# An fp32 product by Strassen's seven half-size products, in four column tiles of TensorE

## The chip, the cores and the metric

One core of a Trainium2 chip. The time is the device time of one execution in microseconds.

## The reference

```python
# x: (8, 4096, 192), weight: (8, 7); w_in: (192, 2048), w_out: (2048, 192); all fp32
w   = softmax(weight, axis=-1)
out = causal 7-tap convolution of x along the sequence, one filter per group of 24 channels
h   = out.reshape(32768, 192) @ w_in
g   = h * sigmoid(1.702 * h)
y   = g @ w_out                       # (32768, 192)
```

The two products are 25.8 billion multiply-adds, and both have to be fp32.

## The kernel before

VectorE makes the convolution for the next step while TensorE works on this one. A step has 1024 tokens: 512 of each half of the batch, one half on partitions 0 to 63 and the other on 64 to 127. The hidden product of this step and the output product of the step before are interleaved, both in row tiles of 64 rows. ("Tile" has two senses here: a buffer that the tile framework hands out from a pool, and a row or column tile, a part of TensorE's array.)

```python
TOK = 512; NF = 16; NC = 3; D = 192           # N_ST = 32 steps
psum_h = ctx.enter_context(tc.tile_pool(name="psum_h", bufs=2, space=PSUM))
psum_o = ctx.enter_context(tc.tile_pool(name="psum_o", bufs=2, space=PSUM))
...
def hidden(s, u):
    ph = psum_h.tile([P, 2, TOK], F32, name="ph")
    for c in range(NC):
        for h in range(2):
            nc.tensor.matmul(ph[:, h, :], w_in_s[halves[h], c, fc * P : (fc + 1) * P],
                             cts[s][halves[h], c, :], start=(c == 0), stop=(c == NC - 1))
    nc.scalar.activation(gs[s][:, fc, :, :], ph, AF.Gelu_apprx_sigmoid)

def output(s, u):                              # 16 such pieces a step
    ...
    if part == 0 and u % 2 == 0:
        acc[z2] = psum_o.tile([P, 2, TOK], F32, name="po")
    for fc in range(u % 2 * (NF // 2), (u % 2 + 1) * (NF // 2)):
        for a in range(2):
            nc.tensor.matmul(po[:, z, 0:D], gs[s][halves[a], fc, h, ...],   # stationary: tokens
                             w_out_s[halves[a], fc, :], ...)                # moving: 192 columns
    if part == 1 and u % 2 == 1:
        nc.vector.tensor_copy(osb[:, b : b + 2, :], po[:, :, 0:D])
        ...                                    # one store for 512 tokens
```

The output's accumulators are tiles of two PSUM banks, and the pool has two of them. While VectorE empties one, TensorE fills the other.

## Time and profile before

| | before |
|---|---|
| time | 2727.88 us (2727.16 to 2728.6) |
| TensorE busy | 98% of the span |
| a step of 1024 tokens | 83.46 us, of which hidden 41.3, output 41.6, the step's border 0.6 |
| first hidden product starts, second step starts | 32.6 us, about 94 us |

The lines behind this table stand in the prediction. A line of the costliest groups reads: line, engine, operation, tiles, shapes, count | busy us and mean ns of one | idle us before them and who ended it. A line of the chain reads: start us, duration us, what. PE is TensorE, PEld its weight loads, DVE VectorE, ACT ScalarE.

### The profile page before, as it was taken

What the parts mean: (1) busy time and instruction counts of PE and PEld (TensorE: products, weight loads), DVE (VectorE), ACT (ScalarE), POOL (GpSimd) and SP (SyncE); (2) the same over time, 40 slices, a digit from 0 to 9 for tenths busy, and PEclk for the clock granted to TensorE, in tenths of its full rate; (3) what the DMA queues carried; (4) which work ended last, traced back from release to release, by engine and by line L of the source; (5) the groups of instructions that cost most, each with busy time, mean ns of one, the idle gap of its engine ahead of it and who ended that gap; (6) DMA issues with size and microseconds to landing.
All of it is one profiled execution on the core that took longest, in us unless ns stands there. A gap on an engine that the chain in (4) does not pass through costs nothing.

```text
span 2725.4 us, 46647 instructions
## 1 busy us (share of the span) xinstructions
PE 2668.3 (98%) x22278; PEld 1927.5 (71%) x22278; DVE 638.7 (23%) x1001; ACT 533.6 (20%) x524; POOL 5.3 (0%) x15
## 2 busy tenths in 40 slices
PE   4999999999999999999999999999999999999999
PEld 2577777777777777777777777777777777777778
DVE  8412222122121222221221212222212222122200
ACT  2211211111111111111112111111111111111210
POOL 0000000000000000000000000000000000000000
PEclk9999999999999999999999999999999999999999
DMA  6111011110111110111101111101111011110000
GB/s 150 20 32 32 7 32 32 26 32 13 26 32 26 32 32 7 32 32 26 32 13 26 32 26 32 27 12 32 32 26 32 7 32 32 26 32 13 7 13 18
DMA packets 104045, 76.39 MB, mean 28 GB/s; under 512 B 3312, under 2 KB 101616, under 8 KB 103856
## 3 DMA queue, kind: packets, MB, share of 16 engines
q1 hardware_dynamic: 103072, 70.27, 12.0%
q8 instruction: 174, 2.85, 0.4%
q0 software_dynamic: 768, 3.15, 0.4%
q14 instruction: 15, 0.12, 0.0%
q10 hardware_dynamic: 16, 0.00, 0.0%
HBM read 48.23 MB, written 25.17 MB: 27 GB/s over the span
## 4 chain that ended last, share of the span: by engine, by line
PE 94%; DVE 5%; issue 0%; DMA 0%; SPq 0%; DVEq 0%
PE po L260 47%; PE ph L235 45%; DVE ct L224 2%; PE po L269 2%; DVE osb L277 1%; DVE g L161 0%; DVE g L154 0%; DMA xin<-in_x_dram 0%; DVE g L160 0%; DVE g L159 0%; DVE w_in_s L166 0%; DVE xt L207 0%; DVE g L158 0%; DVE g L152 0%; DVE g L153 0%
## 5 line engine op out<-in xcount | busy, mean ns | idle before, releaser
L260 PEld LDWEIGHTS po<-w_out_s,g 64*128 64x128 f32 x15872 | 1321.4, 187 | 234.3 <-issue 234.3
L235 PE MATMUL ph<-ct,w_in_s 64*128 64x512 f32 x6144 | 1417.1, 592 | 48.3 <-DVE w_in_s L166 26.3
L260 PE MATMUL po<-w_out_s,g 64*128 64x192 f32 x15872 | 1373.0, 323 | 0.0
L235 PEld LDWEIGHTS ph<-ct,w_in_s 64*128 64x128 f32 x6144 | 578.5, 188 | 554.4 <-issue 476.8
L242 ACT ACTIVATE g<-ph 128x1024 f32<-128x1024 f32 x512 | 524.3, 1024 | 2104.5 <-PE ph L235 2104.5
L277 DVE COPY osb<-po 128x384 f32<-128x384 f32 x128 | 71.3, 557 | 2057.1 <-PE po L260 2017.5
L224 DVE SCALAR_TENSOR_TENSOR ct<-xt,cw,ct 128x512 f32<-128x512 f32 x576 | 431.8, 750 | 16.0
L207 DVE STREAM_TRANSPOSE xt<-xin 128x512 f32<-128x512 f32 x96 | 60.5, 679 | 3.3 <-DMA xin<-in_x_dram 3.2
L222 DVE TENSOR_SCALAR ct<-xt,cw 128x512 f32<-128x512 f32 x96 | 45.0, 469 | 0.0
L269 PE MATMUL po<-w_out_s,g 128*128 128x192 f32 x256 | 41.9, 326 | 0.0
L269 PEld LDWEIGHTS po<-w_out_s,g 128*128 128x128 f32 x256 | 41.6, 190 | 0.2 <-issue 0.2
L179 ACT COPY w_in_s<-w_in_s 64x768 f32<-64x768 f32 x8 | 6.6, 830 | 37.9 <-DVE w_in_s L166 37.8
L154 DVE SCALAR_TENSOR_TENSOR g<-g 128x768 f32<-128x768 uint32 x8 | 7.7, 958 | 0.3
L161 DVE SCALAR_TENSOR_TENSOR g<-g 128x768 uint32<-128x768 uint32 x8 | 7.7, 958 | 0.3
L166 DVE SCALAR_TENSOR_TENSOR w_in_s<-g 64x768 f32<-64x768 f32 x8 | 7.6, 953 | 0.3
L195 PE MATMUL po<-e,sel 8*128 8x7 f32 x6 | 1.4, 354 | 4.9 <-DVE e L192 4.9
L195 PEld LDWEIGHTS po<-e,sel 8*128 8x128 f32 x6 | 1.3, 320 | 4.8 <-issue 4.8
L205 DVE COPY xt<-xt 128x18 f32<-128x18 f32 x28 | 4.7, 167 | 0.0
L160 DVE TENSOR_SCALAR g<-g 128x768 uint32<-128x768 uint32 x8 | 4.5, 560 | 0.3
L159 DVE TENSOR_SCALAR g<-g 128x768 uint32<-128x768 uint32 x8 | 4.5, 560 | 0.3
L158 DVE TENSOR_SCALAR g<-g 128x768 uint32<-128x768 uint32 x8 | 4.4, 554 | 0.0
L153 DVE TENSOR_SCALAR g<-g 128x768 uint32<-128x768 uint32 x8 | 4.4, 552 | 0.0
(19 smaller groups left out, 18.1 us busy)
## 6 DMA issues: line engine op xcount, KB each, us to landing
xin<-in_x_dram SPq DMA_DIRECT2D x128, 320.0 KB, 6.1
out_dram<-osb SPq DMA_DIRECT2D x62, 384.0 KB, 2.6
g<-in_moe_w_in_dram SPq DMA_DIRECT2D x8, 384.0 KB, 22.2
g<-in_moe_w_out_dram POOLq DMA_DIRECT2D x4, 768.0 KB, 16.7
out_dram<-osb SPq DMA_DIRECT2D x4, 192.0 KB, 2.0
w<-in_weight_dram ACTq DMA_DIRECT2D x1, 0.2 KB
```

The lines of the kernel that those rows point to most:

```text
L154: vec.scalar_tensor_tensor(out=m.bitcast(F32), in0=m_lo, scalar=2.0**-24, in1=m_hi, op0=ALU.mult, op1=ALU.add)
L161: vec.scalar_tensor_tensor(out=e, in0=hi, scalar=1 << 31, in1=e, op0=ALU.bitwise_and, op1=ALU.bitwise_or)
L166: vec.scalar_tensor_tensor(out=dst, in0=m[rows, :].bitcast(F32).rearrange("p (c n) -> p c n", c=c), scalar=2.0**-20, in1=e[rows, :].bitcas ...
L179: nc.scalar.copy(w_in_s[halves[1 - h], :, cols[h]], w_in_s[halves[h], :, cols[h]])
L207: nc.vector.transpose(xts[s][:, c, PAD:].rearrange("p (j t) -> p j t", t=Q), xins[s][:, :, c * R : c * R + Q],)
L222: nc.vector.tensor_scalar_mul(dst, src, tap)
L224: nc.vector.scalar_tensor_tensor(out=dst, in0=src, scalar=tap, in1=dst, op0=ALU.mult, op1=ALU.add)
L235: nc.tensor.matmul(ph[:, h, :], w_in_s[halves[h], c, fc * P : (fc + 1) * P], cts[s][halves[h], c, :], start=(c == 0), stop=(c == NC - 1),)
L242: nc.scalar.activation(gs[s][:, fc, :, :], ph, AF.Gelu_apprx_sigmoid)
L260: nc.tensor.matmul(po[:, z, 0:D], gs[s][halves[a], fc, h, (b + z) * P : (b + z + 1) * P], w_out_s[halves[a], fc, :], start=(part == 0 and ...
L269: nc.tensor.matmul(po[:, part, 0:D], gs[s][:, fc, h, (b + part) * P : (b + part + 1) * P], w_out_s[:, fc, :], start=(fc == 0), stop=(fc == ...
L277: nc.vector.tensor_copy(osb[:, b : b + 2, :], po[:, :, 0:D])
```

## The change

Its intent: the output product as 2 x 2 blocks (the tokens in two halves by batch, the 2048 hidden units and the 192 outputs in two halves each) by Strassen's scheme in Winograd's form, with 7 block products in place of 8. That is 1/8 fewer multiply-adds in the output product, still in fp32. For this the output weights become the stationary operand, in column tiles of 32: 96 outputs fill three tiles, and the fourth takes a quarter of the tokens for all three slices. The sums of g that the scheme needs, and the combinations of the products, are VectorE's. A step is now 512 tokens, first a hidden phase, then an output phase.

```diff
-    TOK = 512
+    T = 256;  TA = 3 * T // 4;  TB = T - TA;  TOK = 2 * T          # 64 steps of 512 tokens
-    psum_o = ctx.enter_context(tc.tile_pool(name="psum_o", bufs=2, space=bass.MemoryType.PSUM))
+    psum_o = ctx.enter_context(tc.tile_pool(name="psum_o", bufs=1, space=bass.MemoryType.PSUM))
...
+    def sums_g(s):
+        g = [gs[s][:, i, :, :] for i in range(NS)]
+        yield nc.vector.tensor_sub(g[T1], g[B12], g[B11])          # 128 x 2048 each
+        yield nc.vector.tensor_sub(g[T3], g[B22], g[B12])
+        yield nc.vector.tensor_sub(g[T2], g[B22], g[T1])
+        yield nc.vector.tensor_sub(g[T4], g[T2], g[B21])
...
+    def output(s, others):
+        po = psum_o.tile([P, NR, TOK], F32, name="po")             # NR = 4 banks, one tile
+        def product(a, b, bank, at, first=True):
+            dst = po[:, bank, at : at + TA]
+            for j in range(NK):                                    # 8 chunks
+                for c in range(3):
+                    nc.tensor.matmul(dst[c * Q : (c + 1) * Q, :],
+                        w_out_s[:, a, j, c * Q : (c + 1) * Q], g[:, b, j, 0:TA], ...)
+                for c in range(3):
+                    nc.tensor.matmul(dst[3 * Q :, c * TB : (c + 1) * TB],
+                        w_out_s[:, a, j, c * Q : (c + 1) * Q], g[:, b, j, TA:T], ...)
+            return dst
+        p1 = product(A11, B11, 0, 0)
+        next(others, None)                                         # one of the sums
+        vec.tensor_copy(u1, p1)
+        next(others, None)
+        p6 = product(S2, T2, 1, 0)
+        vec.tensor_add(u2, u1, p6)
+        next(others, None)
+        c11 = product(A12, B21, 0, 0, first=False)
+        turn(0, 0, c11)                                            # turn: 32x32 transposes
+        p7 = product(S3, T3, 2, 0)
+        vec.tensor_add(u3, u2, p7)
+        next(others, None)
+        p5 = product(S1, T1, 3, 0)
+        vec.tensor_add(v, u3, p5)
+        turn(1, 1, v)
+        vec.tensor_add(u2, u2, p5)
+        p3 = product(S4, B22, 1, TA)
+        vec.tensor_add(u2, u2, p3)
+        turn(0, 1, u2)
+        p4 = product(A22, T4, 2, TA)
+        vec.tensor_sub(u3, u3, p4)
+        turn(1, 0, u3)
...                                                                # 24 stores
+            if s == 1:                                             # after the second hidden phase
+                for i in range(NW):
+                    round_w_out(i)
+                sums_w_out()
```

(Left out: index changes of the hidden product, the scratch of the weight rounding, the stores.)

More of the change, by code (lines that the diff above doesn't have):

```diff
@@ L46 @@
     HF = F // 2
-    TOK = 512
-    NB = TOK // P
+    HD = D // 2
+    T = 256
+    TA = 3 * T // 4
+    TB = T - TA
+    TOK = 2 * T
     NJ = TOK // Q
     NF = F // P
+    NK = NF // 2
     PAD = K - 1
     CHUNKS = S // TOK
-    N_ST = (B // 2) * CHUNKS
+    N_BIG = (B // 2) * CHUNKS
+    N_ST = 2 * N_BIG
     XW = D - Q
-    assert B % 2 == 0 and D == NC * R and S % TOK == 0 and F % P == 0 and NF == 4 * NB
+    assert B % 2 == 0 and D == NC * R and HD == 3 * Q and S % TOK == 0 and F % (2 * P) == 0
     x_v = x.rearrange("(h p) s d -> h p s d", h=2)
@@ L64, with load_x @@
     g_pool = ctx.enter_context(tc.tile_pool(name="g", bufs=2))
+    u_pool = ctx.enter_context(tc.tile_pool(name="u", bufs=1))
     osb_pool = ctx.enter_context(tc.tile_pool(name="osb", bufs=2))
     psum_h = ctx.enter_context(tc.tile_pool(name="psum_h", bufs=2, space=bass.MemoryType.PSUM))
-    psum_o = ctx.enter_context(tc.tile_pool(name="psum_o", bufs=2, space=bass.MemoryType.PSUM))
+    psum_o = ctx.enter_context(tc.tile_pool(name="psum_o", bufs=1, space=bass.MemoryType.PSUM))
     ctx.enter_context(tc.manual_schedule())
-    xins, xts, cts, gs, acc = {}, {}, {}, {}, {}
+    xins, xts, cts, gs = {}, {}, {}, {}
     halves = [slice(0, R), slice(R, P)]
-    def load_x(s):
-        p, c = divmod(s, CHUNKS)
+    def load_x(big):
+        p, c = divmod(big, CHUNKS)
         xin = xin_pool.tile([P, NJ, XW], F32, name="xin")
@@ L86, in load_x, with new_g @@
                 )
-        xins[s] = xin
+        xins[big] = xin
+    NS = 7
+    B11, B12, B21, B22, T1, T2, T4 = range(NS)
+    T3 = B12
+    def new_g():
+        return g_pool.tile([P, NS, NK, T], F32, name="g")
     NW = 4
@@ L94 @@
     PIECE = NC * FW
-    assert PIECE == CW * D and 2 * NW * 2 * PIECE + 4 * PIECE <= NF * 2 * TOK
-    scratch = g_pool.tile([P, NF, 2, TOK], F32, name="g").rearrange("p f h t -> p (f h t)").bitcast(U32)
-    raw = scratch[:, 0 : 2 * NW * 2 * PIECE].rearrange("p (i n) -> p i n", i=2 * NW)
-    tmp = scratch[:, 2 * NW * 2 * PIECE : 2 * NW * 2 * PIECE + 4 * PIECE].rearrange(
-        "p (i n) -> p i n", i=4
-    )
+    assert PIECE == CW * D and FW == 2 * P and (NW * 2 + 4) * PIECE <= NS * NK * T
+    scratch = new_g().rearrange("p s f t -> p (s f t)").bitcast(U32)
+    raw = scratch[:, 0 : NW * 2 * PIECE].rearrange("p (i n) -> p i n", i=NW)
+    tmp = scratch[:, NW * 2 * PIECE : (NW * 2 + 4) * PIECE].rearrange("p (i n) -> p i n", i=4)
     w8 = consts.tile([H, K], F32)
@@ L109 @@
     w_in_s = consts.tile([P, NC, F], F32)
-    w_out_s = consts.tile([P, NF, D], F32)
     w_in_v = moe_w_in.bitcast(U32).rearrange("(c q) (h f) -> h q c f", q=R, h=2)
@@ L118 @@
             nc.sync.dma_start(out=piece[halves[h], :, :], in_=w_in_v[h, :, :, cols])
-    fc_order = [
-        (h * HF + i * FW) // P + j for i in range(NW) for h in range(2) for j in range(FW // P)
-    ]
+    A11, A12, A21, A22, S1, S2, S4 = range(NS)
+    S3 = A21
+    w_out_s = consts.tile([P, NS, NK, HD], F32)
     sel = consts.tile([H, NC, P], F32)
@@ L138 @@
             )
-    for i in range(NW):
-        nc.gpsimd.dma_start(
-            out=raw[:, NW + i, :].rearrange("p (c d) -> p c d", c=CW),
-            in_=w_out_v[:, i * CW : (i + 1) * CW, :],
-        )
     def round_piece(i, dsts):
@@ L163, in round_piece @@
         )
-        for rows, dst in dsts:
-            c = dst.shape[1]
+        for rows, c, cols, dst in dsts:
             vec.scalar_tensor_tensor(
                 out=dst,
-                in0=m[rows, :].bitcast(F32).rearrange("p (c n) -> p c n", c=c),
+                in0=m[rows, :].bitcast(F32).rearrange("p (c n) -> p c n", c=c)[:, :, cols],
                 scalar=2.0**-20,
-                in1=e[rows, :].bitcast(F32).rearrange("p (c n) -> p c n", c=c),
+                in1=e[rows, :].bitcast(F32).rearrange("p (c n) -> p c n", c=c)[:, :, cols],
                 op0=ALU.mult,
@@ L176, in round_w_in, with load_w_out, sums_w_out @@
         cols = [slice(h * HF + i * FW, h * HF + (i + 1) * FW) for h in range(2)]
-        round_piece(i, [(halves[h], w_in_s[halves[h], :, cols[h]]) for h in range(2)])
+        round_piece(
+            i, [(halves[h], NC, slice(0, FW), w_in_s[halves[h], :, cols[h]]) for h in range(2)]
+        )
         for h in range(2):
             nc.scalar.copy(w_in_s[halves[1 - h], :, cols[h]], w_in_s[halves[h], :, cols[h]])
-    def round_w_out(i):
-        round_piece(NW + i, [(slice(0, P), w_out_s[:, i * CW : (i + 1) * CW, :])])
+    def load_w_out():
+        for i in range(NW):
+            nc.sync.dma_start(
+                out=raw[:, i, :].rearrange("p (c d) -> p c d", c=CW),
+                in_=w_out_v[:, i * CW : (i + 1) * CW, :],
+            )
+    def round_w_out(i):
+        k, j = divmod(i * CW, NK)
+        round_piece(
+            i,
+            [
+                (slice(0, P), CW, slice(m * HD, (m + 1) * HD), w_out_s[:, 2 * m + k, j : j + CW, :])
+                for m in range(2)
+            ],
+        )
+    def sums_w_out():
+        a = [w_out_s[:, i, :, :] for i in range(NS)]
+        nc.vector.tensor_add(a[S1], a[A21], a[A22])
+        nc.vector.tensor_sub(a[S3], a[A11], a[A21])
+        nc.vector.tensor_sub(a[S2], a[S1], a[A11])
+        nc.vector.tensor_sub(a[S4], a[A12], a[S2])
     nmax = consts.tile([H, 1], F32)
@@ L192 @@
     nc.vector.tensor_scalar_mul(e8, e8, esum)
-    pw = psum_o.tile([P, 2, TOK], F32, name="po")[:, 0, 0 : NC * K].rearrange("p (c k) -> p c k", c=NC)
+    NR = 4
+    pw = psum_o.tile([P, NR, TOK], F32, name="po")[:, 0, 0 : NC * K].rearrange(
+        "p (c k) -> p c k", c=NC
+    )
     for c in range(NC):
@@ L197, with transpose_x, conv @@
     nc.vector.tensor_copy(cw, pw)
-    def transpose_x(s, c):
+    def transpose_x(big, c):
         if c == 0:
-            xt = xts[s] = xt_pool.tile([P, NC, PAD + TOK], F32, name="xt")
-            if s % CHUNKS == 0:
+            xt = xts[big] = xt_pool.tile([P, NC, PAD + TOK], F32, name="xt")
+            if big % CHUNKS == 0:
                 nc.vector.memset(xt[:, :, 0:PAD], 0.0)
             else:
-                nc.vector.tensor_copy(xt[:, :, 0:PAD], xts[s - 1][:, :, TOK : PAD + TOK])
-            xts.pop(s - 1, None)
+                nc.vector.tensor_copy(xt[:, :, 0:PAD], xts[big - 1][:, :, TOK : PAD + TOK])
+            xts.pop(big - 1, None)
         nc.vector.transpose(
-            xts[s][:, c, PAD:].rearrange("p (j t) -> p j t", t=Q),
-            xins[s][:, :, c * R : c * R + Q],
+            xts[big][:, c, PAD:].rearrange("p (j t) -> p j t", t=Q),
+            xins[big][:, :, c * R : c * R + Q],
         )
         if c == NC - 1:
-            xins.pop(s)
-    def conv(s, i):
+            xins.pop(big)
+    def conv(big, i):
         c, k = divmod(i, K)
         if i == 0:
-            cts[s] = ct_pool.tile([P, NC, TOK], F32, name="ct")
-        src = xts[s][:, c, k : k + TOK]
-        dst = cts[s][:, c, :]
+            cts[big] = ct_pool.tile([P, NC, TOK], F32, name="ct")
+        src = xts[big][:, c, k : k + TOK]
+        dst = cts[big][:, c, :]
         tap = cw[:, c, k : k + 1]
@@ L226, in conv, with prepare @@
             )
+    def prepare(big):
+        for c in range(NC):
+            yield lambda c=c: transpose_x(big, c)
+        if big + 1 < N_BIG:
+            yield lambda: load_x(big + 1)
+        for i in range(NC * K):
+            yield lambda i=i: conv(big, i)
     def hidden(s, u):
-        fc = fc_order[u]
+        i, k = divmod(u, 2)
         if u == 0:
-            gs[s] = g_pool.tile([P, NF, 2, TOK], F32, name="g")
-        ph = psum_h.tile([P, 2, TOK], F32, name="ph")
-        for c in range(NC):
-            for h in range(2):
-                nc.tensor.matmul(
-                    ph[:, h, :],
-                    w_in_s[halves[h], c, fc * P : (fc + 1) * P],
-                    cts[s][halves[h], c, :],
-                    start=(c == 0),
-                    stop=(c == NC - 1),
-                )
@@ L242, in hidden @@
-        nc.scalar.activation(gs[s][:, fc, :, :], ph, AF.Gelu_apprx_sigmoid)
-    def output(s, u):
-        quad, part, z2 = u // 8, u % 8 // 4, u % 4 // 2
-        pair = 2 * quad + z2
-        h, b = divmod(2 * pair, NB)
-        if part == 0 and u % 2 == 0:
-            acc[z2] = psum_o.tile([P, 2, TOK], F32, name="po")
-            if b == 0:
-                acc["osb"] = osb_pool.tile([P, NB, D], F32, name="osb")
-        po, osb = acc[z2], acc["osb"]
-        for fc in range(u % 2 * (NF // 2), (u % 2 + 1) * (NF // 2)):
-            if s < N_ST - 1:
-                for a in range(2):
-                    z = a ^ part
-                    nc.tensor.matmul(
-                        po[:, z, 0:D],
-                        gs[s][halves[a], fc, h, (b + z) * P : (b + z + 1) * P],
-                        w_out_s[halves[a], fc, :],
-                        start=(part == 0 and fc == 0),
-                        stop=(part == 1 and fc == NF - 1),
-                    )
-            else:
-                nc.tensor.matmul(
-                    po[:, part, 0:D],
-                    gs[s][:, fc, h, (b + part) * P : (b + part + 1) * P],
-                    w_out_s[:, fc, :],
-                    start=(fc == 0),
-                    stop=(fc == NF - 1),
-                )
-        if part == 1 and u % 2 == 1:
-            nc.vector.tensor_copy(osb[:, b : b + 2, :], po[:, :, 0:D])
-            p, c = divmod(s, CHUNKS)
-            n = 2 if s == N_ST - 1 else NB
-            if (b + 2) % n == 0:
-                t = c * TOK + (b + 2 - n) * P
-                nc.sync.dma_start(
-                    out=out_v[h, p, t : t + n * P, :].rearrange("(b q) d -> q b d", q=P),
-                    in_=osb[:, b + 2 - n : b + 2, :],
-                )
@@ L287 @@
-    NT = NC * K
-    for c in range(NC):
-        transpose_x(0, c)
-    load_x(1)
-    for i in range(NT):
-        conv(0, i)
+            gs[s] = new_g()
+        ph = psum_h.tile([P, 2, 2, T], F32, name="ph")
+        ct = cts[s // 2]
+        t = s % 2 * T
+        for j in range(2):
+            f = k * HF + (2 * i + j) * P
+            for c in range(NC):
+                for h in range(2):
+                    nc.tensor.matmul(
+                        ph[:, h, j, :],
+                        w_in_s[halves[h], c, f : f + P],
+                        ct[halves[h], c, t : t + T],
+                        start=(c == 0),
+                        stop=(c == NC - 1),
+                    )
@@ new lines, in hidden, with turn @@
+        nc.scalar.activation(
+            gs[s][:, 2 * k : 2 * k + 2, 2 * i : 2 * i + 2, :], ph, AF.Gelu_apprx_sigmoid
+        )
+    def sums_g(s):
[5 more added lines that the diff above has]
+    def output(s, others):
+        g = gs.pop(s)
+        po = psum_o.tile([P, NR, TOK], F32, name="po")
+        u = u_pool.tile([P, 4, TA], F32, name="u")
+        osb = osb_pool.tile([P, 2, 2, TA], F32, name="osb")
+        def product(a, b, bank, at, first=True):
+            dst = po[:, bank, at : at + TA]
+            for j in range(NK):
+                for c in range(3):
+                    nc.tensor.matmul(
+                        dst[c * Q : (c + 1) * Q, :],
+                        w_out_s[:, a, j, c * Q : (c + 1) * Q],
+                        g[:, b, j, 0:TA],
+                        start=(first and j == 0),
+                        stop=(j == NK - 1),
+                        skip_group_check=True,
+                    )
+                for c in range(3):
+                    nc.tensor.matmul(
+                        dst[3 * Q :, c * TB : (c + 1) * TB],
+                        w_out_s[:, a, j, c * Q : (c + 1) * Q],
+                        g[:, b, j, TA:T],
+                        start=(first and j == 0 and c == 0),
+                        stop=(j == NK - 1),
+                        skip_group_check=True,
+                    )
+            return dst
+        vec = nc.vector
+        u1, u2, u3, v = (u[:, i, :] for i in range(4))
+        def turn(m, n, src):
+            vec.transpose(
+                osb[:, m, n, :].rearrange("p (j d) -> p j d", d=Q),
+                src.rearrange("p (j t) -> p j t", t=Q),
+            )
+        p1 = product(A11, B11, 0, 0)
[20 more added lines that the diff above has]
+        turn(1, 0, u3)
+        big, odd = divmod(s, 2)
+        p, c = divmod(big, CHUNKS)
+        t = c * TOK + odd * T
+        for n in range(2):
+            rows = out_v[n, p, t : t + T, :].rearrange("(j i) d -> i j d", i=Q)
+            for m in range(2):
+                for c in range(3):
+                    d = slice(m * HD + c * Q, m * HD + (c + 1) * Q)
+                    nc.sync.dma_start(
+                        out=rows[:, 0 : TA // Q, d],
+                        in_=osb[c * Q : (c + 1) * Q, m, n, :].rearrange("i (j d) -> i j d", d=Q),
+                    )
+                    nc.sync.dma_start(
+                        out=rows[:, TA // Q :, d],
+                        in_=osb[3 * Q :, m, n, c * TB : (c + 1) * TB].rearrange(
+                            "i (j d) -> i j d", d=Q
+                        ),
+                    )
@@ L293 @@
+    for work in prepare(0):
+        work()
     round_w_in(0)
+    todo = []
     for s in range(N_ST + 1):
-        for u in range(NF):
-            if s < N_ST:
-                hidden(s, u)
-            if s > 0:
-                output(s - 1, u)
-            if s + 1 < N_ST:
-                if u < NB:
-                    if s == 0 and u + 1 < NW:
-                        round_w_in(u + 1)
-                    if u < NC:
-                        transpose_x(s + 1, u)
-                    if u == NC and s + 2 < N_ST:
-                        load_x(s + 2)
-                else:
-                    if s == 0 and u - NB < NW:
-                        round_w_out(u - NB)
-                    n = NF - NB
-                    for i in range((u - NB) * NT // n, (u - NB + 1) * NT // n):
-                        conv(s + 1, i)
+        if s < N_ST:
+            if s % 2 == 0 and s // 2 + 1 < N_BIG:
+                todo = list(prepare(s // 2 + 1))
+            n = -(-len(todo) // (2 - s % 2))
+            now, todo = todo[:n], todo[n:]
+            for u in range(NK):
+                hidden(s, u)
+                if s == 0 and u % 2 == 1 and u // 2 + 1 < NW:
+                    round_w_in(u // 2 + 1)
+                if s == 0 and u == NK - 1:
+                    load_w_out()
+                for work in now[u * n // NK : (u + 1) * n // NK]:
+                    work()
+            if s == 1:
+                for i in range(NW):
+                    round_w_out(i)
+                sums_w_out()
+        others = sums_g(s) if s < N_ST else iter(())
@@ L315 @@
         if s > 0:
-            gs.pop(s - 1)
-        cts.pop(s, None)
+            output(s - 1, others)
+        for _ in others:
+            pass
 _INS = ['x', 'weight', 'moe_w_in', 'moe_w_out']
```

## The prediction

> **What bounds the kernel now.** I read the page's busy shares first, then the costliest groups, the chain of waits in one step, the waits of TensorE, and two short stretches of the timeline.
>
> ```profile
> PE 2668.3 (98%) x22278; PEld 1927.5 (71%) x22278; DVE 638.7 (23%) x1001; ACT 533.6 (20%) x524; POOL 5.3 (0%) x15
> ...
> L235 PE MATMUL ph<-ct,w_in_s 64*128 64x512 f32 x6144 | 1417.1, 592 | 48.3 <-DVE w_in_s L166 26.3
> L260 PE MATMUL po<-w_out_s,g 64*128 64x192 f32 x15872 | 1373.0, 323 | 0.0
> ...
> L224 DVE SCALAR_TENSOR_TENSOR ct<-xt,cw,ct 128x512 f32<-128x512 f32 x576 | 431.8, 750 | 16.0
> ...
> L154 DVE SCALAR_TENSOR_TENSOR g<-g 128x768 f32<-128x768 uint32 x8 | 7.7, 958 | 0.3
> ...
> q8 instruction: 174, 2.85, 0.4%
> ```
>
> TensorE is busy 98% of the span and every other engine under a quarter. Both products are about half of it. The count 6144 is twice what the loops issue (32 steps x 96): an fp32 matmul is two instructions here. A busy PE need not be a PE at its rate, so the chain inside one step comes next:
>
> ```profile
> 2591.09 2.58 PE ph L235 x12
> 2593.67 2.62 PE po L260 x32
> 2596.29 0.02 issue
> 2596.32 0.56 DVE osb L277
> 2596.88 0.67 DVE ct L224
> 2597.55 0.02 issue
> 2597.57 0.76 DVE ct L224
> 2598.34 0.04 issue
> 2598.38 1.13 PE ph L235 x4
> 2599.51 2.60 PE po L260 x32
> 2602.11 2.58 PE ph L235 x12
> ```
>
> Two row tiles of 64 run side by side, so 12 matmuls of 512 columns are 6 in sequence, 430 ns each; 32 of 192 columns are 16 in sequence, 162.6 ns each. The difference, 267 ns for 320 columns, gives 0.834 ns a column and 2.5 ns fixed. PE streams almost without gaps: no wait can be removed, only columns. A step of 1024 tokens is 16 x (2.58 + 2.60) = 82.9 us, and the lines from 2596.29 to 2598.38 (PE out of work for most of a microsecond at a step's border) bring it to 83.46 us.
>
> ```profile
> PE ph L235 <- DVE w_in_s L166: 26.3, 1, 26.3
> PE ph L235 <- DVE ct L224: 16.1, 29, 4.0
> ...
> 2678.75 0.68 PEld L260 LDWEIGHTS po<-w_out_s,g 64*128 64x128 f32 x8
> 2679.66 1.44 PEld L269 LDWEIGHTS po<-w_out_s,g 128*128 128x128 f32 x9 [0.22 <-issue]
> ```
>
> The first wait is the start: the first hidden matmul begins at 32.6 us, and the second step only at about 94 us, since VectorE rounds weights meanwhile. 32 x 83.46 = 2671 us; the start and the end are the remaining 55 us or so. The last two lines are the only change of tile shape in this kernel, from 64-row to 128-row tiles, and I use it below.
>
> **What the Trainium skill says.**
> 1. "TensorE: Matmul & The Clock Gate", section "LDWEIGHTS (loading the stationary operand)": the load takes about columns / 1.2 in ns, whatever the rows. For 128 columns that is 107 ns; the modelled 187 ns of the trace don't contradict it, because matmuls of 162 ns follow each other without a gap behind them. For 32 columns: 27 ns.
> 2. Same page, "Wait — 56ns, not 53.3ns?": about 2.5 ns fixed per warm matmul (the trace agrees: 2.5), a floor of about 25 ns from start to start for small ones, and about 62 ns each if the sequencer's ucode decodes them. In this trace a load and a matmul come every 81 ns, so nothing here shows which floor applies.
> 3. "TensorEngine Tiling (Array Packing)", section "Key Properties": changing the tiling mode drains TensorE. The trace agrees: at 2679.66 the new mode's load starts only after the last old matmul has streamed, and its matmul waits for that load, where the old one would have followed at once: about 0.2 us a change (0.09 us late, then 0.11 us of load).
> 4. The TensorE page, "Measured speedup vs the span model": three column tiles of 32 ran 2.38 times as fast as in sequence. No column tile is in this trace.
>
> **The change part by part.** Steps are now 512 tokens (256 of each half), 64 of them, each a hidden phase then an output phase.
>
> Hidden: the same columns in matmuls of 256: 96 in sequence x (256 x 0.834 + 2.5 = 216 ns) = 20.7 us a step, 1327 us in all, against 32 x 16 x 2.58 = 1321 us. No gain.
>
> Output, removed: 32 x 41.6 = 1331 us. Added: seven products, each over 8 chunks of 128 of the halved hidden dimension, each chunk giving 96 x 256 outputs: three column tiles stream 192 tokens, the fourth streams 64 tokens three times. With two instructions per fp32 matmul, tiles 0 to 2 carry 7 x 8 x 2 = 112 matmuls of 162.6 ns = 18.2 us; tile 3 carries 336 of 64 x 0.834 + 2.5 = 55.9 ns = 18.8 us. I take 18.8, if the four run side by side. In all 64 x 18.8 = 1203 us: 128 us less than now. Exactly 7/8 would be 166 us; the small fourth tile loses 38.
>
> Tile shapes: two changes per step x 0.2 us x 64 = 26 us added. The step-border waits of about 0.6 us x 31 = 18 us should go, because the convolutions now end well ahead in the odd steps.
>
> DVE: four sums of 128x2048 elements per step. From 958 ns for 768 elements and 750 for 512 (1.25 to 1.46 ns an element[...]) I take 2.2 to 2.8 us each, 9 to 11 us a step. The evacuation (seven operations and four transposes of 192 columns, some 0.35 us each) is 4 us, the convolutions 8.5. Together about 23 of 40 us: DVE goes from 23% to nearly 60% but stays hidden. Its one dangerous place is the A12 x B21 product, which accumulates into the bank whose first content must be copied out first. That copy comes in DVE's order after one sum: the sum starts 1 us into the phase, so the copy ends at about 4 us, and PE reaches that product at 5.4. No wait.
>
> ACT: 8 activations of 1.02 us a step, hidden. DMA: 128-byte rows on the output make about 3070 packets a step[...]. Hidden, except at the end: 18 issues of some 0.4 us after the last transpose, so the tail grows from 4 to 12 us.
>
> Start: the second hidden phase reuses the buffer in which the output weights are rounded, so its activations wait for that. DVE's order: first-phase work with three weight pieces ends at about 63 us, first sums at 75, the rest of the convolutions at 84, four output pieces of 5.7 us at 107. Then the hidden phase resumes: first output at about 124 us, where head plus two hidden phases would be 74. Before, this loss was 20 us; it becomes 50. So 30 us are given back here.
>
> Sum: 124 (first two hidden phases) + 64 x 18.8 + 62 x 20.7 + 126 x 0.2 + 12 = 124 + 1203 + 1283 + 25 + 12 = 2647 us of span, about 2650 as time. From the other side: -128 - 18 + 6 + 26 + 30 + 8 = -76 us, 2652. I say **2655 us**.
>
> **The rivals.**
> (a) *PE's issue becomes the bound.* Now 4 instructions (loads and matmuls) come in 162.6 ns, 40 ns each. Afterwards it is 24 in 336 ns, 14 ns each. If the limit were 20 ns an instruction, a chunk would take 480 ns, a phase 26.9 us, and 64 x 8.1 = 518 us are added: about 3170. At 16 ns: 384 ns, 21.5 us, about 2830. At 62 ns per matmul: 744 ns and about 4100. For it: nothing in the trace comes near such a rate. Against it: the instruction fetch is only 174 blocks for the whole program, 0.4% of the DMA time, and would grow to about 430; and loads and matmuls cannot both cost 62 ns, as four now fit in 162.6.
> (b) *Column tiles load or stream one after another.* If the 12 loads of a chunk serialize at 27 ns plus 2.5 each, they take 354 ns against 336: 64 us more, about 2720, within 2%. If the streams serialize, the output is three to four times as long, over 5000 us; the skill's 2.38 speaks against that.
> (c) *Tile 3 hides its small load better or worse.* If its fixed cost vanished, 18.2 us would hold: 38 us less, about 2617. If each of its matmuls lost 10 ns, 3.4 us a step: 2870.
> (d) *DVE becomes the path*, if in-place sums and PE's reads slow each other so that a sum takes over 4 us. I give it little.
>
> **Range and chances.** The mechanism gives 2615 to 2655 if column tiles run freely, just past the 2% border at 2673. Small issue costs land it between 2673 and 2782, a real issue limit above. The gain is small because 166 us of Strassen meet some 90 us of tile loss, drains and start. Range **2600 to 2900**. Chances: faster 0.52, within 2% 0.22, slower 0.26.
>
> **What would show it.** Right: hidden stretches of about 20.7 us and output stretches near 18.8 us with four column tiles overlapping, 0.2 us between them, the first output near 124 us, DVE at 55 to 60% without a wait of PE on it after the start. Wrong: an output stretch well over 19 us with PE not waiting for any engine (then issue or loads), a matmul of tile 3 spaced more than 56 ns apart, PE waiting on u or on the sums, or the output weights' rounding not delaying the second phase.

## More of the kernel before

The kernel before took 2727.88 us (median of 2 runs), and 2727.31 and 2727.28 us (7 runs each, on two chips) beside the later experiments, so the experiments can be compared with each other.

## The result, and the profile after

The changed kernel takes 2938.94 us (2938.9 to 2938.98, 2 runs): slower. The ratio to before is 1.0774 (95% interval 1.0727 to 1.082). Ratios in this document are the mean time of one kernel's fast runs over that of the other's in the same rounds, so not quite the ratio of the medians quoted.

The busy shares and the groups of the changed kernel, by line (L286 is the hidden product, L316 column tiles 0 to 2, L326 the fourth tile):

```profile
PE 2637.6 (90%) x55302; PEld 2411.5 (82%) x55302; DVE 1396.2 (48%) x1841; ACT 533.6 (18%) x524; POOL 2.2 (0%) x11
...
L316 PE MATMUL po<-g,w_out_s 128*32 128x192 f32 x21504 | 1254.8, 328 | 215.9 <-DVE u L360 70.3
...
L300 DVE TENSOR_TENSOR g<-g 128x2048 f32<-128x2048 f32 x64 | 146.7, 2292 | 659.7 <-ACT g L293 659.7
```

TensorE was busy 98% before and is 90% now. The new idle time stands in front of the output's matmuls, and VectorE ends it, although VectorE is busy for less than half of the span. TensorE's waits (us in total, times, longest) tell which VectorE instructions those are:

```profile
PE po L316 <- DVE u L360: 70.3, 64, 1.1
PE ph L286 <- ACT g L293: 35.4, 1, 35.4
PE po L316 <- DVE osb L340: 30.4, 64, 0.5
PE po L316 <- DVE u L347: 28.8, 64, 0.5
PE po L316 <- DVE u L362: 28.7, 64, 0.4
PE po L316 <- DVE u L350: 28.7, 64, 0.4
PE po L316 <- DVE u L355: 28.6, 64, 0.4
```

Six different instructions, each 64 times, once per step: the copy of P1 (L347), the additions of P6, P7, P5 and P3 (L350, L355, L360, L362) and the transpose of C11 (L340). Each is the last VectorE instruction that reads one product. So TensorE waits after every product but the last. The chain of waits shows it inside one step (of the many short TensorE pieces only a few are shown):

```profile
1302.49 20.92 PE ph L286 x192
1323.41 0.19 PE po L316
1326.06 0.18 PE po L326 x3
1326.26 0.37 DVE u L347
1326.68 0.26 PE po L316
1329.40 0.18 PE po L326 x3
1329.60 0.36 DVE u L350
1330.01 0.26 PE po L316
...
1339.43 0.18 PE po L326 x3
1339.63 0.36 DVE u L358
1340.02 0.38 DVE osb L340
1340.40 0.25 DVE u L360
1340.69 0.26 PE po L316
```

A product runs for 2.83 us, from 1323.41 to 1326.24. Then VectorE works for 0.37 us, then the next product starts. P6 (from 1326.68) goes into bank 1 and VectorE has just read bank 0, so nothing in the arithmetic asks for this wait. After P5 three VectorE instructions lie on the chain, because two of them read P5 and a transpose stands between them in VectorE's order. From the start of P6 to the start of the next product it is 3.33 us (1330.01 - 1326.68), where eight chunks of 0.336 us need 2.69: each wait costs about 0.65 us. The picture repeats in every step, at a period of 44.43 us.

The idle times in the list of waits add up to 215.5 us, which is less than what the waits cost. The ends of matmuls are modelled (one of the fourth tile is drawn 219 ns long, although the next starts 56 ns after it), so the idle time begins late in the profile. The distance between starts is the better measure: from the first to the last matmul start of an output phase it is 23.36 us in the trace, where 18.8 were predicted. The difference of 4.56 us in 64 steps is 292 us.

### The profile page after: what moved, and what is told of

Same layout as the page of the kernel before. It is cut to its first block, busy times and chain, and to the rows that moved or that the text cites. A ratio compares the mean times of both kernels' runs of the same rounds, so it can differ in the third digit from the quotient of the medians.

```text
span 2937.3 us, 115577 instructions
## 1 busy us (share of the span) xinstructions
PE 2637.6 (90%) x55302; PEld 2411.5 (82%) x55302; DVE 1396.2 (48%) x1841; ACT 533.6 (18%) x524; POOL 2.2 (0%) x11
## 4 chain that ended last, share of the span: by engine, by line
PE 89%; DVE 8%; issue 1%; DMA 1%; SPq 0%; ACT 0%; ACTq 0%
PE ph L286 46%; PE po L326 26%; PE po L316 18%; DVE osb L340 2%; DVE u L362 1%; DVE u L355 1%; DVE u L358 1%; DVE u L347 1%; DVE u L350 1%; DVE u L360 1%; DMA xin<-in_x_dram 0%; DMA g<-in_moe_w_in_dram 0%; DVE ct L261 0%; ACT g L293 0%; DVE g L173 0%
## 5 line engine op out<-in xcount | busy, mean ns | idle before, releaser
L316 PE MATMUL po<-g,w_out_s 128*32 128x192 f32 x21504 | 1254.8, 328 | 215.9 <-DVE u L360 70.3
L286 PE MATMUL ph<-ct,w_in_s 64*128 64x256 f32 x12288 | 1351.4, 378 | 67.7 <-ACT g L293 35.4
L286 PEld LDWEIGHTS ph<-ct,w_in_s 64*128 64x128 f32 x12288 | 1189.0, 188 | 210.7 <-ACT g L293 35.8
L326 PE MATMUL po<-g,w_out_s 128*32 128x64 f32 x21504 | 1284.6, 220 | 0.0
L326 PEld LDWEIGHTS po<-g,w_out_s 128*32 128x32 f32 x21504 | 1212.2, 110 | 0.0
L316 PEld LDWEIGHTS po<-g,w_out_s 128*32 128x32 f32 x21504 | 834.7, 109 | 299.0 <-DVE u L360 80.6
L300 DVE TENSOR_TENSOR g<-g 128x2048 f32<-128x2048 f32 x64 | 146.7, 2292 | 659.7 <-ACT g L293 659.7
L303 DVE TENSOR_TENSOR g<-g 128x2048 f32<-128x2048 f32 x64 | 146.2, 2285 | 0.0
L302 DVE TENSOR_TENSOR g<-g 128x2048 f32<-128x2048 f32 x64 | 146.2, 2285 | 0.0
L301 DVE TENSOR_TENSOR g<-g 128x2048 f32<-128x2048 f32 x64 | 146.0, 2281 | 0.3 <-ACT g L293 0.3
L362 DVE TENSOR_TENSOR u<-u,po 128x192 f32<-128x192 f32 x64 | 22.7, 355 | 190.7 <-PE po L326 190.7
L355 DVE TENSOR_TENSOR u<-u,po 128x192 f32<-128x192 f32 x64 | 22.6, 354 | 190.8 <-PE po L326 190.8
L365 DVE TENSOR_TENSOR u<-u,po 128x192 f32<-128x192 f32 x64 | 22.7, 354 | 164.3 <-PE po L326 164.3
L347 DVE COPY u<-po 128x192 f32<-128x192 f32 x64 | 22.9, 358 | 131.7 <-PE po L326 131.7
L340 DVE STREAM_TRANSPOSE osb<-u 128x192 f32<-128x192 f32 x192 | 72.6, 378 | 6.6
L340 DVE STREAM_TRANSPOSE osb<-po 128x192 f32<-128x192 f32 x64 | 24.5, 382 | 52.0 <-PE po L326 49.1
L350 DVE TENSOR_TENSOR u<-u,po 128x192 f32<-128x192 f32 x64 | 22.7, 354 | 52.3 <-PE po L326 52.3
L358 DVE TENSOR_TENSOR u<-u,po 128x192 f32<-128x192 f32 x64 | 22.6, 353 | 52.0 <-PE po L326 52.0
## 6 DMA issues: line engine op xcount, KB each, us to landing
g<-in_moe_w_out_dram SPq DMA_DIRECT2D x4, 768.0 KB, 11.5
```

The source lines that it names most:

```text
L286: nc.tensor.matmul(ph[:, h, j, :], w_in_s[halves[h], c, f : f + P], ct[halves[h], c, t : t + T], start=(c == 0), stop=(c == NC - 1),)
L300: yield nc.vector.tensor_sub(g[T1], g[B12], g[B11])
L301: yield nc.vector.tensor_sub(g[T3], g[B22], g[B12])
L302: yield nc.vector.tensor_sub(g[T2], g[B22], g[T1])
L303: yield nc.vector.tensor_sub(g[T4], g[T2], g[B21])
L316: nc.tensor.matmul(dst[c * Q : (c + 1) * Q, :], w_out_s[:, a, j, c * Q : (c + 1) * Q], g[:, b, j, 0:TA], start=(first and j == 0), stop=(j ...
```

## The experiments

Theory A: the tile framework puts accesses to one tile in order as a whole. The four banks are one tile here, so a product may not start before VectorE has read the product before it. Rival B: VectorE comes late, because the sums of g keep it busy. Rival C: the restart of the column tiles (drain, weight loads, the issue of 24 short instructions per chunk) costs the time itself, and the wait only stands there.

**Four tiles.** The accumulators become four tiles of one bank; the instructions and their addresses stay (banks 4 to 7 in both built programs).

```diff
-        po = psum_o.tile([P, NR, TOK], F32, name="po")
+        po = [psum_o.tile([P, TOK], F32, name=f"po{i}") for i in range(NR)]
-            dst = po[:, bank, at : at + TA]
+            dst = po[bank][:, at : at + TA]
```

> The changed kernel with one edit: the output's PSUM tile of four banks becomes four tiles of one bank each; the same instructions otherwise, right result. Theory A (the tile framework orders accesses by whole tile, so each product waits until VectorE has read the product before it, although the two lie in different banks): the six waits of a step, five of about 0.65 us and one of 1.3, go: 64 x 4.56 = 292 us less than 2939, about 2650. Rival B (VectorE is late because of the sums of g, so the waits are real): about 2900 or more. Rival C (restarting the column tiles at each product costs the time by itself: drain, weight loads, instruction issue): above 2850.

Measured: 2649.31 us (2647.61 to 2649.66, 4 runs), the right result, ratio to before 0.9712 (0.9696 to 0.9729). TensorE's waits of that run, complete:

```profile
PE ph L286 <- ACT g L293: 35.4, 1, 35.4
PE ph L286 <- DVE w_in_s L177: 26.8, 1, 26.8
PE ph L286 <- ACT w_in_s L192: 5.1, 3, 2.0
PE po L232 <- DVE e L226: 4.7, 1, 4.7
```

All waits of the steady state are gone, those that are left belong to the start. Busy times in one step of the changed kernel and of this one (columns: stretch, length, busy us and count of TensorE, weight loads, VectorE, ScalarE, GpSimd, then clock, DMA share, GB/s):

```profile
1302.42:1346.85 44.43, 41.06 (x867) 37.59 (x865) 20.66 (x28) 8.19 (x8) 0.00 (x0) 1.00 0.24 41
```

```profile
1299.90:1339.72 39.82, 39.82 (x866) 37.15 (x864) 21.05 (x28) 8.19 (x8) 0.00 (x0) 1.00 0.08 12
```

VectorE does the same work in both, 20.7 and 21.1 us; only the step is shorter by 4.61 us. 64 x 4.61 = 295 us, and the times differ by 289.6; most of the rest is small stalls of the four-tile run, taken up below with the fourth column tile. Theory A holds, B and C fall: the products change here too, with the same loads and the same short instructions, and that costs nothing visible. What lies in a wait of 0.65 us beside the 0.37 us of VectorE was not taken apart.

**Two tiles.** Banks 0 and 1 in one tile, 2 and 3 in the other. It asks whether the waits follow the tiles one by one.

```diff
+        po = [psum_o.tile([P, 2, TOK], F32, name=f"po{i}") for i in range(2)]
+            dst = po[bank // 2][:, bank % 2, at : at + TA]
```

> Two PSUM tiles of two banks, banks 0 and 1 in one, 2 and 3 in the other. Theory A: the waits before P6, the A12 x B21 product and P5 stay (3 x 0.65 us), those before P7, P3 and P4 go (2.6 us a step): 2939 - 64 x 2.6 = about 2770. Rivals B and C: no change, 2900 or more.

Measured: 2769.00 us in one look, right result. The waits that stay are the three foretold, and no other of the six:

```profile
PE po L316 <- DVE u L347: 28.7, 64, 0.5
PE po L316 <- DVE u L350: 28.6, 64, 0.4
PE po L316 <- DVE u L355: 28.5, 64, 0.4
```

An output phase lasts 20.71 us from first to last matmul start, against 18.75 with four tiles: three waits of 0.65 us. The built programs agree: of the matmuls of an output phase, 7 carry a wait on VectorE with one tile, 5 with two tiles and 4 with four. The 4 that stay ask for work that was done long before, since no wait of the steady state shows in that trace.

**No sums.** The four sums of g are left out and products read other quarters of g (a wrong result), with one PSUM tile as in the change.

```diff
-        others = sums_g(s) if s < N_ST else iter(())
+        others = iter(())
-        p6 = product(S2, T2, 1, 0)
+        p6 = product(S2, B21, 1, 0)          # P5 and P4 likewise
```

> The changed kernel without the four sums of g on VectorE (products read other quarters of g in their place; a wrong result on purpose), one PSUM tile as in the changed kernel. Theory A: VectorE was idle before each evacuation anyway, so 2939 less at most the 9 us that the first sums hold up the start: 2925 to 2940. Rival B (the sums make VectorE late): over 100 us less.

Measured: 2926.88 us in one look. Its busy shares:

```profile
PE 2636.9 (90%) x55302; PEld 2410.5 (82%) x55302; DVE 826.9 (28%) x1585; ACT 534.0 (18%) x524; POOL 2.2 (0%) x11
```

VectorE has 570 us less to do, TensorE is as busy as before, and the period of a step stays at 44.42 us. The 12 us come from the start alone: the first output product begins at 112.0 us instead of 123.7 (at most 9 us were expected there). Rival B is out.

**A doubled evacuation, with one tile and with four.** The copy of P1 out of PSUM is issued twice. This puts a price on one VectorE instruction in each arrangement.

```diff
         vec.tensor_copy(u1, p1)
+        vec.tensor_copy(u1, p1)
```

> The changed kernel with the copy of P1 out of PSUM done twice. Theory A: in one PSUM tile every evacuation lies on TensorE's path, so a second copy of about 0.37 us costs 64 x 0.37 = 24 us: about 2963. If evacuations were hidden: 2939.

> The same doubled copy in four_tiles. Theory A: it is hidden beside TensorE, 2649 within 5 us.

Measured: 2963.60 us with one tile, 24.7 more than the change, which is 64 x 0.386 us; and 2652.49 us with four tiles, 3.2 more than the median there. In the traces a step grows from 44.43 to 44.82 us with one tile and stays at 39.82 with four. The same instruction is paid in full in one arrangement and lies beside TensorE's work in the other.

**The fourth column tile.** With four tiles, it does two instead of three matmuls in six of the eight chunks (wrong). It asks what sets the pace inside a product.

```diff
-                for c in range(3):
+                for c in range(3 if j == 0 or j == NK - 1 else 2):
                     nc.tensor.matmul(
                         dst[3 * Q :, c * TB : (c + 1) * TB],
```

> Four tiles, and the fourth column tile does two of its three matmuls in six of eight chunks (a wrong result on purpose). If the fourth tile with 3 x 55.9 ns a pass sets the pace of a product, as predicted, against 162.6 ns of the others, this gives 7 x 8 x 2 x (167.7 - 162.6 ns) = 0.57 us a step, at most 37 us less than four_tiles: about 2615. If instruction issue or weight loads set the pace, a chunk of 20 in place of 24 instructions gains up to a sixth of the output, 200 us: about 2450.

Measured: 2606.25 us in one look, 43 us less than four tiles, where the expectation said at most 37. In the chain two hidden phases follow each other at 39.25 us:

```profile
1318.81 20.92 PE ph L286 x192
1358.07 20.92 PE ph L286 x192
```

That is 0.57 us less than the 39.82 us of four tiles (both medians of the starts), just what was worked out; 64 x 0.57 = 36 us. The output phase from first to last start falls by 0.67 us (18.75 to 18.08), but that count leaves out the last matmul, 162.6 ns long now and 55.9 before. The reading stands: the fourth tile paces a product by its three fixed costs. A limit of issue would have brought more: the expectation's 200 us hold for all eight chunks, and for six of eight it is 150.

About 4 us of the rest are stalls that the prediction did not have. In the four-tile trace 21 output matmuls start 0.05 to 0.3 us late, with no other engine to wait for, and the steps lose 4.2 us to such stalls in all. All 21 stand at the same place of a block of 256 TensorE instructions; the program's loads and matmuls, 55,302 of each, arrive in 432 fetches (queue q8), 256 in each on average. In this run, with a sixth fewer instructions in six of eight chunks, every step takes 39.25 us and there is none. So at 24 instructions in 336 ns the supply of instructions now and then runs late. This is read from the place of the stalls; no run tested it.

**A version that beats both.** Besides the four tiles: g in three tiles, the output weights loaded early and rounded during the first hidden phase, the first step's convolutions moved into the first output phase, and stores in the order in which their data is ready, in the last step on two queues. These edits came together and were not tried one by one.

```diff
-        return g_pool.tile([P, NS, NK, T], F32, name="g")
+        return [g_pool.tile([P, n, NK, T], F32, name=f"g{i}") for i, n in enumerate((2, 2, 3))]
...
-            if s == 1:
+            if s == 0:
                 for i in range(NW):
                     round_w_out(i)
                 sums_w_out()
+        if s == 1:
+            others = first_others(late, others)      # convolutions first, then the sums
...
-        for n in range(2): ... for m in range(2):
+        for m, n in ((0, 0), (1, 1), (0, 1), (1, 0)):
```

> Right result. Four PSUM tiles, and three edits outside the steady state: g in three tiles instead of one, so that the second hidden phase does not wait for the rounding of the output weights; the output weights are loaded early and rounded during the first hidden phase, the convolutions for the next step move into the first output phase; the stores go out in the order in which their data is ready, those of the last step on two queues. From the trace of four_tiles: the second hidden phase loses 35.4 us to the wait for the rounding, and the tail is 11.5 us. If both go as planned, the third hidden phase starts at about 112 us instead of 147 and the tail halves: 2649 - 35 - 6 = about 2608. Rival: VectorE is the bound of the start anyway and the work only moves: 2635 or more.

Measured: 2610.49 us (2610.43 to 2614.13, 4 runs), right result, ratio to before 0.9575 (0.9559 to 0.9591). Its waits of TensorE, the longest ones:

```profile
PE ph L293 <- DVE w_in_s L191: 27.7, 3, 26.7
PE po L239 <- DVE e L233: 4.7, 1, 4.7
PE po L329 <- DVE g L309: 4.5, 1, 4.5
```

The wait of 35.4 us for ScalarE, behind which ScalarE waited for the rounded output weights, is gone. In the chain of four tiles the third hidden phase starts at 142.05 (the 147 of the expectation is the start with one tile), and in this kernel at 108.69:

```profile
104.49 1.03 ACT g L293
105.57 17.58 PE ph L286 x144
142.05 20.92 PE ph L286 x192
```

```profile
108.69 20.92 PE ph L293 x192
```

The tail, from the last matmul start to the end, shrinks from 11.5 us with four tiles to 4.8 us. Start and tail bring 33.4 + 6.7 = 40.1 us, and the spans of the two profiled runs differ by 37.1: stalls of the kind just described take 6.8 us here, where they took 4.2. The rival, that VectorE is the bound of the start anyway and the work only moves, falls for the 33.4 us. The first output phase is now 9.9 us longer than a later one, with the wait of 4.5 us for the sums in it; what is left of the start was not taken apart further.

## Why the prediction was wrong, point by point

**The step that failed** is in the part on DVE: "Its one dangerous place is the A12 x B21 product, which accumulates into the bank whose first content must be copied out first. [...] No wait." The prediction looked for waits in the data: which product needs which bank emptied. It found one, and there it was right: with four tiles that copy ends 3.3 us into the phase, before the 5.4 us at which its product comes. But the order in the program comes from tiles, and the change had put the accumulators, which took turns in two tiles before, into one tile of four banks. So six waits of 0.65 us, the one after P5 twice as long, stand in every step: 4.61 us x 64 = 295 us, more than the 128 us that the columns save. With that falls the other half of the step, that VectorE "stays hidden": at 48% busy it held up six of seven products. None of the rivals named it, though "PE waiting on u" stood among the signs of being wrong, and that sign came. Rival (d) had VectorE on the path, but by slow sums; the sums took 2.28 to 2.29 us, and leaving them out changed no step. The two-tile and four-tile runs and the doubled copy show the cause by removing it in two doses and by pricing one instruction. What was not looked at is the framework's own rule: that it goes by whole tiles is inferred from these runs and from the waits in the built programs. A second buffer for the one tile was not tried; all six waits stand between products of one step, within one and the same tile, so it would hardly have removed them.

**The other steps held, with small slips.**
- Output phase without waits: predicted 18.8 us, measured 18.75 from first to last start (four tiles). The fourth tile's matmuls start every 56 ns; 55.9 were predicted.
- Hidden phase: predicted 20.7 us and 0.2 us for the change of tile shape; the chain has 20.92. The whole step: 18.8 + 20.7 + 0.4 = 39.9 predicted, 39.82 measured. The two changes of tile shape cost some 0.3 us together, not 0.4 (39.82 less 20.74 and 18.78 of streaming).
- Start: first output predicted at 124 us, measured at 123.7. Tail: predicted 12 us, measured 11.5.
- VectorE: predicted 23 us of a step, measured 21.1. For a sum the two rates that the prediction quotes give 2.6 to 3.0 us, not its 2.2 to 2.8; 2.28 to 2.29 were measured. The first sum starts 1.4 us before the output phase, not 1 us into it. The loads and stores stayed hidden.
- Rivals (a) and (b), issue or serial weight loads: a chunk of 24 instructions takes the predicted 0.336 us. Of (a) there is a small sign, the stalls of 4.2 us in all.
- The sum, 2655 us, is 0.2% from what the same instructions take with four tiles, 2649 us. A little of that is luck: the stalls and the cheaper changes of shape nearly cancel.

So the mechanism of the gain was right, and so was its small size. The missing term was one of about 290 us that no count of instructions contains.

## What to carry to other kernels

When a change merges accumulators into one tile, count the waits that the framework will put in, not only those that the data needs: compare which instructions carry waits in the built program before and after. A busy share that falls on the bounding engine, with many equal short waits on an engine that is mostly idle, points to such an order, and splitting the tile is a cheap test. Gaps between starts tell what such waits cost; idle times behind modelled ends told a quarter too little here (215 of 295 us).

## What the Trainium skill lacked or had wrong

- "TensorE: Matmul & The Clock Gate", section "Wait — 56ns, not 53.3ns?", gives two floors for small matmuls, about 25 ns from start to start and about 62 ns where the ucode decodes them, but none for loads and matmuls in column tiles together. Here 12 matmuls and 12 loads were sustained in 336 ns, a matmul every 28 ns, so the 62 ns did not bind.
- "Runtime: NRT & Kernel Launch", section "Instruction fetch mechanics", speaks of an issue floor of about 20 cycles per instruction, which is 16.7 ns at the 1.2 GHz that the TensorE page gives the sequencer. Here TensorE's instructions came every 14.0 ns over whole output phases, so a floor of that size did not bind these loads and matmuls; with four tiles 21 of them came 0.05 to 0.3 us late, all at one place of a block of 256.
- The TensorE page, section "Measured speedup vs the span model", has three column tiles at 2.38 times, and no figure for four. Here an fp32 matmul was two instructions of 0.834 ns a column plus 2.5 ns each, and four column tiles ran side by side: a chunk whose matmuls would take 6 x 162.6 + 6 x 55.9 = 1311 ns in sequence took 336 ns, 3.9 times less.
- No page says that accumulators in different banks serialize with their evacuation when they are one tile of the framework: 4.61 us of a 44.43 us step here. "PSUM — Partial Sum Buffer" names bank and quadrant as what has to be guarded; the four-tile run, with TensorE in one bank and VectorE in another, gave right results.
